# Another order of work in the lead-in of a chunked scan with a feed-forward layer, one dummy product less, and an earlier place for loads and state copies

## The chip, the cores and the metric

The kernel runs on one core of a Trainium2 chip. A core has five engines that run their own instruction lists in order and wait for each other through semaphores: TensorE (PE, matrix products; PEld is its weight load), VectorE (DVE), ScalarE (ACT), GpSimd (POOL) and SyncE (SP), which here only issues DMA transfers. The metric is the time of one execution in microseconds of the device; the median of several runs is compared.

## The reference

Per batch (4) and head (8), a sequence of 768 steps is run through a decayed linear recurrence in chunks, and its output, 3072 tokens of 256 features, goes through a feed-forward layer of width 2048.

```python
for c in range(nc):
    cum = np.cumsum(la, axis=-1)                       # la = log(a) of the chunk
    L = np.exp(cum[:, :, :, None] - cum[:, :, None, :]) * causal
    M = np.einsum('bhin,bhjn->bhij', Cc, Bc) * L
    y = M @ xc + (Cc @ state) * np.exp(cum)
    state = exp(sum(la)) * state + sum_j(Bc_j x_j * exp(cum[-1] - cum_j))
h = y_all @ w_in
out = np.maximum(0.01 * h, h) @ w_out
```

## The kernel before, in words

The sequence is cut into 16 chunks of 48 steps. For a chunk c the kernel makes the exponents of the decays on TensorE (in the buffer `pd` or `sc`), takes their exponential on ScalarE into `lt` (`decay_exp`, L290 and L295), makes the scores C·B on TensorE (`scores`, L327), multiplies the two on VectorE (`weigh`, L341), lets GpSimd write the decay of the carried state beside them (`state_decay`, L312), and then forms with 64 small products both the outputs of the chunk and its next state (`chunk_products`, L357). The state leaves by a transpose on VectorE into `stage` (`turn`, L387) and eight small copies into the input `xs` of the next chunk (`hand_on`, L403). A tuple of numbers gives the engine of each of the eight: 0 is ScalarE, 1 VectorE, 2 GpSimd. So each chunk waits for the copies of the one ahead of it.

The exponents of chunks 0 to 2 are made directly from `la` (`fill_reach`, L591, on VectorE; `decay_direct`, L263). From chunk 3 on they come from one product (`decay_stack`, L271) of two stacked tables, `dl` and `dr`. Some of their rows are sums of `la`, split into three parts (`split_sums`, L223 to L228), written to DRAM (`save_sums`, L231 and L235) and read back for each chunk (`load_rows`, L244 and L247); the upper rows of `dr` are filled once (`fill_rest`, L203).

The feed-forward layer needs each output in a high and a low part (`highs` on ScalarE, `lows` on VectorE), 512 tokens at a time, and each weight block in a high part `wh` and a low part `wl`. A weight block arrives raw by DMA (`fetch_w`), and five steps make it: `mag` on ScalarE (`decode_abs`, L441), `decode_hold` and `decode_shift` on VectorE (L453, L458), `decode_sign` (L464) and `decode_low` (L473) on VectorE, then `settle`: `wh` on ScalarE (L486) and `wl` on GpSimd (L487). `ahead` runs the next block's `mag` early. The six products of a feed-forward step (`ffn_in`, L518) take the pairs in this order: `xh` with `wh`, `xl` with `wh`, `xh` with `wl`. Then ScalarE and VectorE make the activation and its low part (L525, L528, L531), and a later `ffn_out` (L542) multiplies by the second weights. Step 0 starts when chunk 2's outputs and weight block 0 are there. Steps 1 and 3 carry chunks 3 and 4; they are the ones with `s < EARLY` in the main loop that hand a state on.

The order of all work is that of the Python code: the engines take their instructions in the order in which the code issues them. `keep_warm` (L120) issues dummy products: `WARM` of them at the start and four more ahead of step 1. SP's queue holds a load back until the buffer or the transfer that it needs is free, and everything behind it waits too.

Of the kernel before, what the change touches and what calls it, by code (L numbers as in the profile page):

```python
# [10 lines left out]
F32 = mybir.dt.float32  # L11
# [21 lines left out]
WARM = 4  # L33
# [30 lines left out]
def scan_ffn(ctx: ExitStack, tc: tile.TileContext, a_l, c_l, d_l, x_l, w_l, out_l):  # L64
# [73 lines left out]
    fetch_x(2)  # L138
# [62 lines left out]
    def fill_rest():  # L201
        both = [Q, SLOTS * NM, Q]
        nc.vector.tensor_copy(  # L203
            dr[:Q].rearrange("q b m i -> q (b m) i"), later[:Q].unsqueeze(1).to_broadcast(both)
        )
# [183 lines left out]
    def hand_on(c, by):  # L389
        if c + 1 == NC:  # L390
            return
        stage = stages.pop(c)
        alloc_x(c + 1)
        pairs = [slice(0, 2), slice(2, NB)]
        for g in range(2):
            for p in range(2):
                rows = slice((2 * g + p) * D, (2 * g + p) * D + N)
                for k, bs in enumerate(pairs):
                    copy = (nc.scalar.copy, nc.vector.tensor_copy, nc.gpsimd.tensor_copy)[
                        by[4 * g + 2 * p + k]  # L400
                    ]
                    h = half(g, bs.start)
                    copy(  # L403
                        xss[c + 1][h * R:h * R + N, 2 * p:2 * p + 2, bs], stage[rows, :, bs],
                    )
# [165 lines left out]
    with tc.tile_pool(name="ps_d", bufs=2, space=PSUM, reuse_waits="tile") as ps_d:  # L571
# [26 lines left out]
        def reverse_near(space, at):  # L598
            for k in range(2):
                for g in range(2):  # L600
# [4 lines left out]
                    )  # L605
            nc.scalar.activation(
# [15 lines left out]

        fill_columns()
# [8 lines left out]
        fill_reach(2, 0)  # L632
# [3 lines left out]
        fill_reach(1, 0)  # L636
        next(splitting)
        for _ in splitting:
            pass
        fill_reach(1, 1)  # L640
        save_sums(0)
        load_rows(3)
        load_rows(4)
        fetch_c(3)
# [3 lines left out]
        reverse_near(first, 2 * Q)  # L648
        decay_direct(1, pds[1])
        state_decay(0)  # L650
        weigh(0, sc)
        spread_c(1)
# [3 lines left out]
        for top in tops:  # L656
            nc.gpsimd.memset(top.rearrange("p c h -> p (c h)").bitcast(F32), 0.0)
# [10 lines left out]
        fill_rest()  # L668
# [8 lines left out]
        fetch_w(1, nc.scalar)  # L677
        state_decay(2)
        lows(0, os)
        os = banks()  # L680
# [6 lines left out]
        fetch_x(3)  # L687
        fetch_w(2)
# [18 lines left out]
        state_decay(3)  # L707
# [3 lines left out]
        turn(2, os)  # L711
        decode_abs(2)
# [3 lines left out]
        hand_on(2, (0, 2, 0, 2, 0, 2, 0, 0))  # L716
        decode_hold(2)
        decode_shift(2)
        weigh(3, scs[3])
# [172 lines left out]
    for s in range(total):  # L892
# [29 lines left out]
        if c is not None:  # L922
            os = banks()
            chunk_products(c, os)
            if s < EARLY:
                turn(c, os)
            else:
                states(c, os)
# [11 lines left out]
        if c is not None:  # L940
            highs(c, os)
            if s < EARLY:
# [5 lines left out]
                hand_on(c, (0, 2, 0, 2, 0, 2, 0, 2))  # L948
# [33 lines left out]
        if s == 0:  # L982
            fetch_x(LEAD + 1)
# [98 lines left out]
```

## Time and profile before

| what | us |
|---|---|
| three runs | 307.56, 307.9, 370.02 |
| median | 307.9 |
| the profiled execution | 307.64 |
| its span in the trace | 305.3 |
| TensorE busy in the span | 295.8 |
| VectorE, ScalarE, GpSimd busy | 221.5, 182.4, 71.9 |

The span runs from the first to the last recorded instruction; 2.3 us of the profiled execution lie around it. Busy times are sums over the whole span, in which stages differ much: TensorE is busy without a break through most of it, and with breaks in its first 45 us. The granted clock of TensorE is given in tenths of full speed (2.4 GHz; the lower level is 1.2 GHz).

### The profile page before, as it was taken

The page shows a single profiled execution, that of the slowest core. Times are in us where ns is not written, and L with a number is a line of the kernel's source. Part 1 is how long each engine was busy: PE and PEld are TensorE (multiplying, and loading weights), DVE is VectorE, ACT ScalarE, POOL GpSimd, SP SyncE. Part 2 cuts the span into 40 slices and gives each one's busy share as a digit, 9 for nine tenths or more (in the row PEclk, how much of TensorE's full clock was granted, in tenths as well). Part 3 has the DMA queues.
Part 4 walks back from the last instruction along what each step waited for, and adds up shares of the span by engine and source line. Part 5 has one row for each costly group of instructions (what it writes and reads, how often), then busy time and mean ns, then how long its engine had stood idle before and what let it go on. Part 6 is the DMA issues. An engine that isn't in the chain of part 4 may idle for free.

```text
span 305.3 us, 6817 instructions
## 1 busy us (share of the span) xinstructions
PE 295.8 (97%) x2720; PEld 233.4 (76%) x2720; DVE 221.5 (73%) x395; ACT 182.4 (60%) x348; POOL 71.9 (24%) x149
## 2 busy tenths in 40 slices
PE   8879899999999999999999999999999999999994
PEld 4557677777777777888888888888888888888883
DVE  7898888978786679956877887677665565556552
ACT  7857886766755554845365556673665364536452
POOL 5735676857676430000000000000000000000000
PEclk9979999999999999999999999999999999999999
DMA  7696674585634001000100000000030000000003
GB/s 227 211 298 242 241 253 150 172 243 194 227 101 133 3 2 71 0 2 0 69 3 0 0 0 2 1 0 0 2 127 10 0 3 0 0 0 2 0 0 137
DMA packets 12428, 23.86 MB, mean 78 GB/s; under 512 B 4334, under 2 KB 4718, under 8 KB 12398
## 3 DMA queue, kind: packets, MB, share of 16 engines
q1 hardware_dynamic: 12254, 22.92, 22.3%
q10 hardware_dynamic: 144, 0.52, 0.5%
q8 instruction: 21, 0.34, 0.5%
q14 instruction: 9, 0.07, 0.1%
HBM read 20.00 MB, written 3.44 MB: 77 GB/s over the span
## 4 chain that ended last, share of the span: by engine, by line
PE 85%; POOL 3%; issue 3%; DVE 3%; ACT 2%; DMA 2%; SPq 1%; POOLq 0%; DVEq 0%; ACTq 0%
PE sc L786 18%; PE op L811 14%; PE sc L811 14%; PE op L542 13%; PE hp L518 12%; PE hp L786 7%; PE sc L357 3%; DMA bcn<-c_l 2%; PE sc L327 2%; POOL wl L487 2%; PE sc L271 1%; POOL xs L403 1%; DVE top L464 1%; ACT xs L403 1%; DVE w L473 1%
## 5 line engine op out<-in xcount | busy, mean ns | idle before, releaser
L403 POOL COPY xs<-stage 16x128 f32<-16x128 f32 x99 | 35.4, 357 | 24.8 <-DVE stage L387 16.4
L525 ACT ACTIVATE gh<-hp 128x512 fp32r<-128x512 f32 x32 | 19.1, 597 | 24.3 <-PE hp L518 24.1
L822 ACT ACTIVATE gh<-u 128x512 fp32r<-128x512 f32 x32 | 20.0, 626 | 17.7 <-DVE u L863 17.7
L542 PE MATMUL op<-gh,wh 128*128 128x512 f32 x64 | 27.9, 436 | 0.0
L826 DVE TENSOR_TENSOR gl<-u,gh 128x512 fp32r<-128x512 f32 x32 | 22.0, 687 | 7.9 <-ACT u L823 7.9
L862 DVE TENSOR_TENSOR u<-sc,kept 128x512 f32<-128x512 f32 x16 | 11.1, 692 | 22.2 <-PE sc L786 22.2
L822 ACT ACTIVATE gh<-kept 128x512 fp32r<-128x512 f32 x16 | 10.1, 632 | 28.1 <-DVE kept L871 28.1
L822 ACT ACTIVATE gh<-hp 128x512 fp32r<-128x512 f32 x16 | 9.6, 599 | 26.8 <-PE hp L786 26.8
L871 DVE TENSOR_TENSOR kept<-sc,kept 128x512 f32<-128x512 f32 x16 | 11.1, 692 | 19.5 <-PE sc L786 19.3
L542 PE MATMUL op<-gh,wl 128*128 128x512 f32 x64 | 25.1, 392 | 0.0
L542 PE MATMUL op<-gl,wh 128*128 128x512 f32 x64 | 25.0, 391 | 0.0
L531 DVE TENSOR_TENSOR gl<-hp,gh 128x512 fp32r<-128x512 f32 x32 | 21.7, 679 | 4.5 <-ACT hp L528 4.3
L811 PE MATMUL op<-gh,wh 128*128 128x512 f32 x64 | 24.9, 389 | 0.0
L811 PE MATMUL sc<-gh,wh 128*128 128x512 f32 x64 | 24.9, 389 | 0.0
L811 PE MATMUL sc<-gl,wh 128*128 128x512 f32 x64 | 24.9, 389 | 0.0
L811 PE MATMUL op<-gl,wh 128*128 128x512 f32 x64 | 24.9, 389 | 0.0
L811 PE MATMUL sc<-gh,wl 128*128 128x512 f32 x64 | 24.9, 389 | 0.0
L811 PE MATMUL op<-gh,wl 128*128 128x512 f32 x64 | 24.9, 389 | 0.0
L487 POOL TENSOR_TENSOR wl<-w,wh 128x512 fp32r<-128x512 f32 x16 | 21.1, 1320 | 11.7 <-ACT wh L486 11.4
L341 DVE TENSOR_TENSOR lt<-sc,lt 128x384 f32<-128x384 f32 x32 | 16.3, 551 | 8.9 <-ACT gh L525 7.8
L518 PE MATMUL hp<-xh,wh 128*128 128x512 f32 x64 | 20.8, 407 | 0.2 <-DVE stage L387 0.2
L823 ACT ACTIVATE u<-u 128x512 f32<-128x512 f32 x32 | 20.2, 633 | 1.0
(150 smaller groups left out, 741.6 us busy)
## 6 DMA issues: line engine op xcount, KB each, us to landing
raw<-w_l SPq DMA_DIRECT2D x15, 512.0 KB, 3.8
bcn<-d_l SPq DMA_DIRECT2D x13, 448.0 KB
xs<-x_l SPq DMA_DIRECT2D x16, 256.0 KB, 3.5
out_l<-ob SPq DMA_DIRECT2D x12, 256.0 KB, 2.0
bcn<-c_l SPq DMA_DIRECT2D x3, 352.0 KB
raw<-w_l ACTq DMA_DIRECT2D x1, 512.0 KB
dl<-left_d SPq DMA_DIRECT2D x13, 9.0 KB, 1.6
dr<-right_d SPq DMA_DIRECT2D x13, 9.0 KB
```

What stands on the lines that cost most here:

```text
L341: nc.vector.tensor_tensor(out=to, in0=at, in1=to, op=ALU.mult)
L403: copy(xss[c + 1][h * R:h * R + N, 2 * p:2 * p + 2, bs], stage[rows, :, bs],)
L487: nc.gpsimd.tensor_tensor(out=wl[:, f], in0=w32s[f], in1=wh[:, f], op=ALU.subtract)
L518: nc.tensor.matmul(hp, lhsT=w_half[h][:, f, k * 128:(k + 1) * 128], rhs=x[t][:, k, :], start=(n == 0), stop=(n == 5),)
L525: nc.scalar.activation(ghs[s], hp, AF.Prelu, alpha=0.01)
L531: nc.vector.tensor_tensor(out=gls[s], in0=hps.pop(s), in1=ghs[s], op=ALU.subtract)
L542: nc.tensor.matmul(op, lhsT=w_half[h][:, f, DM + m * 128:DM + (m + 1) * 128], rhs=x, start=(start and i == 0), stop=(last and i == 2),)
L786: nc.tensor.matmul(bank, lhsT=w[h], rhs=x[g], start=start and i == 0, stop=i == 2, skip_group_check=True,)
L811: nc.tensor.matmul(outs[t][m], lhsT=w_half[h][:, f, DM + m * 128:DM + (m + 1) * 128], rhs=x, start=start and i == 0, stop=last and i == 2,)
L822: nc.scalar.activation(gh, h, AF.Prelu, alpha=0.01)
L823: nc.scalar.activation(in_place, h, AF.Prelu, alpha=0.01)
L826: nc.vector.tensor_tensor(out=gl, in0=g, in1=gh, op=ALU.subtract)
```

## The change: what it does

- One dummy product less at the start (`WARM` 3 for 4).
- Up to the products of chunk 1, steps change places. The part of `reverse_near` that is on TensorE goes ahead of the scores of chunk 0, with its exponential (`reverse_near_exp`) behind chunk 0's decay. The second and third part of the split sums go behind, with the save of the sums. The clearing of the two `top` buffers on GpSimd goes ahead of and between two state decays. `fill_rest` goes from one copy on VectorE ahead of chunk 0's transpose to two half copies behind `lows(0)`, the one on VectorE, the other on GpSimd.
- Loads: x of chunk 2 goes behind the save, followed by the input of chunk 3 and weight block 1 (which ScalarE's queue issued before), and only then by the rows of chunks 3 and 4. x of chunk 4 goes ahead of weight block 2.
- State copies: `hand_on` takes a set of engines. For chunks 2, 3 and 4 GpSimd's four copies are issued right behind the transpose and ScalarE's four at the old place. Chunk 2 had five on ScalarE and three on GpSimd. `ahead()` (the `mag` of block 3) is called ahead of ScalarE's copies of chunk 2.

```diff
-WARM = 4
+WARM = 3
...
     fetch_c(2)
-    fetch_x(2)
...
-    def fill_rest():
-        both = [Q, SLOTS * NM, Q]
-        nc.vector.tensor_copy(
-            dr[:Q].rearrange("q b m i -> q (b m) i"), later[:Q].unsqueeze(1).to_broadcast(both)
-        )
+    def fill_rest(b, eng):
+        eng.tensor_copy(dr[:Q, b], later[:Q].unsqueeze(1).to_broadcast([Q, NM, Q]))
...
-    def hand_on(c, by):
+    def hand_on(c, by, engines=(0, 1, 2)):
...
+                    engine = by[4 * g + 2 * p + k]
+                    if engine not in engines:
+                        continue
...
+        def fill_top(i):
+            nc.gpsimd.memset(tops[i].rearrange("p c h -> p (c h)").bitcast(F32), 0.0)
...
-        fill_reach(2, 0)
+        fill_reach(1, 0)
         splitting = split_sums(first)
         next(splitting)
         spread_c(0)
-        fill_reach(1, 0)
-        next(splitting)
-        for _ in splitting:
-            pass
         fill_reach(1, 1)
-        save_sums(0)
-        load_rows(3)
-        load_rows(4)
-        fetch_c(3)
+        reverse_near(first, 2 * Q)
         sc = banks()
         scores(0, sc)
         decay_exp(0, pds[0])
-        reverse_near(first, 2 * Q)
+        reverse_near_exp(first, 2 * Q)
+        next(splitting)
+        fill_reach(2, 0)
         decay_direct(1, pds[1])
+        fill_top(0)
         state_decay(0)
+        fill_top(1)
         weigh(0, sc)
+        for _ in splitting:
+            pass
+        save_sums(0)
+        fetch_x(2)
+        fetch_c(3)
+        fetch_w(1)
+        load_rows(3)
+        load_rows(4)
         spread_c(1)
         decay_exp(1, pds[1])
         spread_c(2)
         state_decay(1)
-        for top in tops:
-            nc.gpsimd.memset(top.rearrange("p c h -> p (c h)").bitcast(F32), 0.0)
...
         fill_reach(2, 1)
-        fill_rest()
...
-        fetch_w(1, nc.scalar)
         state_decay(2)
         lows(0, os)
+        fill_rest(1, nc.vector)
+        fill_rest(0, nc.gpsimd)
...
         fetch_x(3)
+        fetch_x(4)
         fetch_w(2)
...
         settle()
-        state_decay(3)
         decode_hold(1)
         decode_shift(1)
         lows(2, os)
         turn(2, os)
+        hand_on(2, (0, 2) * 4, (2,))
+        state_decay(3)
         decode_abs(2)
         decode_sign(1)
         do_low(1)
         settle()
-        hand_on(2, (0, 2, 0, 2, 0, 2, 0, 0))
         decode_hold(2)
         decode_shift(2)
+        ahead()
+        hand_on(2, (0, 2) * 4, (0,))
...
             if s < EARLY:
                 turn(c, os)
+                hand_on(c, (0, 2) * 4, (2,))
...
                 ahead()
-                hand_on(c, (0, 2, 0, 2, 0, 2, 0, 2))
+                hand_on(c, (0, 2) * 4, (0,))
...
         if s == 0:
-            fetch_x(LEAD + 1)
             fetch_w(max(raws) + 1)
```

The order on VectorE from the tables of chunk 1 to the transpose of chunk 1, before (`reach_137` is chunk 1's table, `reach_138` chunk 2's; `dr<-later` is `fill_rest`):

```order
L591 TENSOR_TENSOR reach_138<-la,upto 112x384
L224 TENSOR_TENSOR rest<-sc,parts 128x192
L591 TENSOR_TENSOR reach_137<-la,upto 112x384
L228 TENSOR_TENSOR parts<-rest,parts 128x4x48
L591 TENSOR_TENSOR reach_137<-la,upto 112x384
L341 TENSOR_TENSOR lt<-sc,lt 128x8x48 x2
L591 TENSOR_TENSOR reach_138<-la,upto 112x384
L203 COPY dr<-later 48x1536
L387 STREAM_TRANSPOSE stage<-pd 128x256
```

and with the change (`reach_134` is chunk 1's table, `reach_135` chunk 2's):

```order
L588 TENSOR_TENSOR reach_134<-la,upto 112x384
L220 TENSOR_TENSOR rest<-sc,parts 128x192
L588 TENSOR_TENSOR reach_134<-la,upto 112x384
L588 TENSOR_TENSOR reach_135<-la,upto 112x384
L337 TENSOR_TENSOR lt<-sc,lt 128x8x48 x2
L224 TENSOR_TENSOR parts<-rest,parts 128x4x48
L588 TENSOR_TENSOR reach_135<-la,upto 112x384
L383 STREAM_TRANSPOSE stage<-pd 128x256
```

The copy into `dr` no longer stands ahead of chunk 0's transpose; the last part of the split sums stands behind the weighing of chunk 0 for ahead of it.

The order on GpSimd from the clearing of `top` to the work of weight blocks 0 to 2, before (the `lt` rows are state decays of chunks 0, 1, 2, 3, 4; the `xs` rows the state copies of chunks 0, 1, 2):

```order
L312 TENSOR_TENSOR lt<-bcn,erev 128x16x16 x2
L657 MEMSET top_167 128x512
L657 MEMSET top_168 128x512
L403 COPY xs<-stage 16x2x64 x4
L312 TENSOR_TENSOR lt<-bcn,erev 128x16x16
L403 COPY xs<-stage 16x2x64 x4
L487 TENSOR_TENSOR wl<-w_423,wh 128x512
L312 TENSOR_TENSOR lt<-bcn,erev 128x16x16
L487 TENSOR_TENSOR wl<-w_493,wh 128x512
L403 COPY xs<-stage 16x2x64 x3
L312 TENSOR_TENSOR lt<-bcn,erev 128x16x16
L487 TENSOR_TENSOR wl<-w_546,wh 128x512
```

and with the change:

```order
L623 MEMSET top_164 128x512
L308 TENSOR_TENSOR lt<-bcn,erev 128x16x16
L623 MEMSET top_165 128x512
L308 TENSOR_TENSOR lt<-bcn,erev 128x16x16
L400 COPY xs<-stage 16x2x64 x4
L308 TENSOR_TENSOR lt<-bcn,erev 128x16x16
L201 COPY dr<-later 48x768
L400 COPY xs<-stage 16x2x64 x4
L484 TENSOR_TENSOR wl<-w_425,wh 128x512
L400 COPY xs<-stage 16x2x64 x4
L308 TENSOR_TENSOR lt<-bcn,erev 128x16x16
L484 TENSOR_TENSOR wl<-w_499,wh 128x512
```

The four copies of chunk 2 now stand ahead of the `wl` of block 1, where three stood behind it; a half of `fill_rest` stands ahead of chunk 1's copies.

SP's queue behind the load of chunk 2's input (the third `bcn<-c_l`), before:

```order
L113 DMA xs<-x_l 128x512
L231 DMA left_d<-parts 128x2x144
L235 DMA right_d<-parts 128x288
L244 DMA dl<-left_d 48x2x48
L247 DMA dr<-right_d 6x16x48
L244 DMA dl<-left_d 48x2x48
L247 DMA dr<-right_d 6x16x48
L105 DMA bcn<-d_l 128x896
L244 DMA dl<-left_d 48x2x48
L247 DMA dr<-right_d 6x16x48
L113 DMA xs<-x_l 128x512
L96 DMA raw<-w_l 128x2048 x2
```

and with the change:

```order
L227 DMA left_d<-parts 128x2x144
L231 DMA right_d<-parts 128x288
L113 DMA xs<-x_l 128x512
L105 DMA bcn<-d_l 128x896
L96 DMA raw<-w_l 128x2048
L240 DMA dl<-left_d 48x2x48
L243 DMA dr<-right_d 6x16x48
L240 DMA dl<-left_d 48x2x48
L243 DMA dr<-right_d 6x16x48
L240 DMA dl<-left_d 48x2x48
L243 DMA dr<-right_d 6x16x48
L113 DMA xs<-x_l 128x512 x2
```

The input of chunk 3 (`bcn<-d_l`), x of chunk 2 and weight block 1 now stand ahead of the rows that are read back.

## Rows read from the trace of the kernel before

**Rows 1.** The page's first part: busy time of the engines in us, share of the span, instructions.

```profile
PE 295.8 (97%) x2720; PEld 233.4 (76%) x2720; DVE 221.5 (73%) x395; ACT 182.4 (60%) x348; POOL 71.9 (24%) x149
```

**Rows 2.** Busy time of each engine by stretch (stretch, its length, then PE, PEld, DVE, ACT, POOL busy with their counts, the granted clock, the share of the DMA engines, GB/s), late stretches.

```profile
33.15:36.00 2.85, 1.94 (x93) 1.53 (x96) 2.38 (x5) 2.83 (x7) 2.65 (x5) 1.00 0.98 361
...
42.30:45.00 2.70, 2.40 (x98) 1.86 (x98) 1.61 (x4) 2.67 (x7) 2.50 (x5) 1.00 0.96 344
45.00:130.00 85.00, 85.00 (x1236) 65.25 (x1235) 69.53 (x130) 54.25 (x108) 44.35 (x98) 1.00 0.37 120
```

**Rows 3.** The same view, the lead-in's second half up to feed-forward step 0.

```profile
10.00:12.00 2.00, 2.00 (x20) 0.94 (x16) 1.96 (x4) 1.84 (x5) 1.72 (x7) 1.00 0.16 43
...
14.00:16.00 2.00, 1.30 (x55) 0.69 (x50) 1.96 (x6) 1.81 (x5) 1.14 (x4) 1.00 1.01 388
16.00:18.00 2.00, 0.83 (x44) 0.51 (x33) 1.84 (x5) 1.22 (x3) 0.00 (x0) 1.00 0.86 272
18.00:20.00 2.00, 1.29 (x29) 1.13 (x29) 1.97 (x7) 0.62 (x1) 1.19 (x1) 0.82 0.83 208
20.00:22.00 2.00, 2.00 (x6) 1.37 (x5) 1.93 (x4) 0.97 (x2) 1.13 (x2) 0.50 1.00 345
```

**Rows 4.** Instructions in order of time (start, duration, engine, line, operation, tile, count; in brackets the idle time ahead and what ended it): TensorE, the dummies at the start and the first part of `reverse_near`.

```profile
1.05 1.89 PE L120 MATMUL sc<-idle 128*128 128x512 bf16 x4 [1.05 <-DVE idle L116]
...
6.95 0.31 PE L602 MATMUL sc<-la,after 48*64 48x24 f32 x8
```

**Rows 5.** The same view, VectorE from chunk 0's transpose to the end of weight block 0.

```profile
8.63 0.97 DVE L203 COPY dr<-later 48x1536 bf16<-48x1536 bf16 x1
...
9.53 0.43 DVE L387 STREAM_TRANSPOSE stage<-pd 128x256 f32<-128x256 f32 x1
...
12.06 0.56 DVE L422 TENSOR_TENSOR xl<-pd,xh 128x384 fp32r<-128x384 f32 x1
13.48 0.45 DVE L387 STREAM_TRANSPOSE stage<-sc 128x256 f32<-128x256 f32 x1 [0.86 <-PE sc L357]
...
17.32 0.69 DVE L473 SCALAR_TENSOR_TENSOR w<-raw,top 128x512 uint32<-128x512 uint32 x1
```

**Rows 6.** The same view, GpSimd.

```profile
5.34 0.40 POOL L194 COPY dl<-sel 6x256 bf16<-6x256 bf16 x1
...
9.13 1.40 POOL L657 MEMSET top<- 128x512 f32 x2
10.59 1.28 POOL L403 COPY xs<-stage 16x128 f32<-16x128 f32 x4
11.95 0.62 POOL L312 TENSOR_TENSOR lt<-bcn,erev 128x256 f32<-128x256 f32 x1
...
18.81 1.27 POOL L487 TENSOR_TENSOR wl<-w,wh 128x512 fp32r<-128x512 f32 x1 [3.48 <-ACT wh L486]
20.04 1.09 POOL L312 TENSOR_TENSOR lt<-bcn,erev 128x256 f32<-128x256 f32 x1
...
31.10 1.29 POOL L487 TENSOR_TENSOR wl<-w,wh 128x512 fp32r<-128x512 f32 x1 [3.00 <-ACT wh L486]
32.46 2.16 POOL L403 COPY xs<-stage 16x128 f32<-16x128 f32 x4
```

**Rows 7.** The same view, ScalarE.

```profile
10.08 0.80 ACT L306 ACTIVATE cs<-bcn,mine 128x192 f32<-128x192 f32 x2 [1.07 <-DMA bcn<-c_l]
...
18.05 0.62 ACT L486 CAST wh<-w 128x512 fp32r<-128x512 f32 x1 [0.33 <-DVE w L473]
...
21.71 0.62 ACT L486 CAST wh<-w 128x512 fp32r<-128x512 f32 x1 [0.93 <-DVE w L473]
22.24 1.57 ACT L403 COPY xs<-stage 16x128 f32<-16x128 f32 x5
...
25.06 0.66 ACT L441 ACTIVATE mag<-raw 128x512 bf16<-128x512 bf16 x1
```

**Rows 8.** The same view, TensorE: chunk 3's scores, the first pair of feed-forward step 0, the last pair of step 1, chunk 4's products.

```profile
17.14 0.38 PE L327 MATMUL sc<-bcn 32*64 32x96 f32 x4 [0.69 <-DMA bcn<-d_l]
18.52 0.88 PE L327 MATMUL sc<-bcn 32*64 32x96 f32 x28 [1.00 <-issue]
...
19.58 1.19 PE L518 MATMUL hp<-xh,wh 128*128 128x512 f32 x2 [0.18 <-DVE stage L387]
...
24.62 0.63 PE L518 MATMUL hp<-xh,wl 128*128 128x512 f32 x2
...
34.33 1.12 PE L357 MATMUL sc<-lt,xs 64*32 64x64 f32 x56 [0.86 <-POOL xs L403]
```

**Rows 9.** The same view, DMA issues (their duration is the issue's).

```profile
11.05 0.32 SPq L244 DMA_DIRECT2D dl<-left_d  x1
...
12.63 0.36 SPq L105 DMA_DIRECT2D bcn<-d_l  x1
```

**Rows 10.** The page's DMA parts: the queue that carries the engines' code (packets, MB, share of 16 engines), and the loads of the `dl` rows (count, KB each, median us from issue to landing).

```profile
q8 instruction: 21, 0.34, 0.5%
...
dl<-left_d SPq DMA_DIRECT2D x13, 9.0 KB, 1.6
```

**Rows 11.** VectorE in order of time, two `decode_sign` (L464): the first with GpSimd idle, the second beside the GpSimd row at 31.10.

```profile
28.83 0.74 DVE L464 SCALAR_TENSOR_TENSOR top<-raw,mag 128x512 uint16<-128x512 uint16 x1
...
31.75 1.25 DVE L464 SCALAR_TENSOR_TENSOR top<-raw,mag 128x512 uint16<-128x512 uint16 x1
```

More of the change, by code (lines that the diff above doesn't have):

```diff
@@ L387, in turn @@
         nc.vector.transpose(stage, by_batch(c, space)[:, :, :, :D])
-    def hand_on(c, by):
+    def hand_on(c, by, engines=(0, 1, 2)):
         if c + 1 == NC:
             return
-        stage = stages.pop(c)
+        stage = stages[c]
         alloc_x(c + 1)
@@ L398, in hand_on @@
                 for k, bs in enumerate(pairs):
-                    copy = (nc.scalar.copy, nc.vector.tensor_copy, nc.gpsimd.tensor_copy)[
-                        by[4 * g + 2 * p + k]
-                    ]
+                    engine = by[4 * g + 2 * p + k]
+                    if engine not in engines:
+                        continue
+                    copy = (nc.scalar.copy, nc.vector.tensor_copy, nc.gpsimd.tensor_copy)[engine]
                     h = half(g, bs.start)
@@ L605, in reverse_near, with reverse_near_exp @@
                     )
+        def reverse_near_exp(space, at):
             nc.scalar.activation(
```

## Prediction

> **What bounds the kernel now.** The first view is the page's busy times: TensorE works in 295.8 of 305.3 us, the others far less [rows 1]. So the question is where its 9.5 us of idle time lie. The second view, stretches, answers: from 45 us on TensorE has no break (85.00 of 85.00 us in the first 85) [rows 2]. No order of work shortens that part; the end moves by what the first 45 us give. Idle time that is left there: 0.91 us between 33.15 and 36, 0.30 between 42.3 and 45 [rows 2], and 6.00 - 1.30 - 0.83 - 1.29 = 2.58 between 14 and 20 [rows 3]. Behind that last idle stretch the granted clock falls to 0.50, the lower of its two levels, in 20 to 22, with 0.82 in the two microseconds ahead [rows 3]; that costs 2 x 0.50 + 2 x 0.18, about 1.4. These large pieces together are 5.2 us. Two per cent of the time, about what a measurement of this kernel can tell from no change, are 6.2. So even a change that won all of them would stay within 2%.
>
> The third view, instructions in order of time, tells what TensorE waits for. In the lead-in it waits for chunk 3's input (0.69) and then, inside 32 products of one kind, 1.00 us for nothing that the profile shows [rows 8]. Step 0 then begins at 19.58 [rows 8], though its `wh` is there at 18.67 [rows 7]. In chunk 4's products it waits for GpSimd's state copies (0.86) [rows 8], which stand behind the `wl` of 31.10, which waited for ScalarE [rows 6]. Behind both is one chain: VectorE makes a weight block, ScalarE its `wh`, GpSimd its `wl`.
>
> The sum is made against the profiled execution, 307.64 us, 0.26 under the median of the three runs.
>
> **The change part by part.**
>
> *One dummy less.* 1.89 / 4 = 0.47 us [rows 4]. Ahead of chunk 0's scores now stand the small `reverse_near` products, 0.31 [rows 4]. At most 0.16 us is left, and the scores wait for ScalarE besides. I take 0.
>
> *VectorE without `fill_rest` ahead of the transpose.* The copy runs from 8.63 to 9.60 and chunk 0's transpose right behind it [rows 5]. That transpose can come a few tenths earlier, but ScalarE then still waits for chunk 2's input until 10.08 [rows 7], whose transfer has the same bytes ahead of it as before, and so `xl` of chunk 0 still comes at 12.06. What can be gained shows at chunk 1's transpose: VectorE is free for it at 12.06 + 0.56 = 12.62, now does its half of the copy (0.97 / 2 = 0.49) and can transpose at 13.11, where it did at 13.48 after a wait for TensorE [rows 5]. TensorE makes chunk 1's products earlier, since GpSimd's copies of chunk 0 (10.59 to 11.87) lose the two clearings (1.40) ahead of them and can follow the transpose at once [rows 6]. Gain 0.37, and VectorE works on without much idle time to the end of weight block 0 at 18.01 [rows 5], which becomes 17.64. Bounds 0 and 0.37.
>
> *GpSimd's half of `fill_rest`.* 768 elements a lane: by the copy of 256 of the same type (0.40) 1.2 us, by the slowest operation on 256 (1.09) 3.3 [rows 6]. The state decay of chunk 2 ahead of it ends at about 11.5 (12.57 less the 1.0 by which chunk 0's copies come earlier). So it ends between 12.7 and 14.8; chunk 1's copies can begin at 13.56. Cost 0 to 1.2; I take 0, by the row of the same type.
>
> *Loads.* Rows for chunk 3 were asked for at 11.05, when the DMA engines stood at 0.16 [rows 3, 9]. Now 256 KB of x, 448 KB of chunk 3's input and 512 KB of weights are ahead in the queue: 1216 KB at the 388 GB/s of a full stretch [rows 3] are 3.1 us. If these begin at about 10.5 (the save now follows the weighing of chunk 0), they end at 13.6, and the rows land between 14.2 and 15.2 (1.6 us from issue to landing [rows 10] is the upper end). Chunk 2's products need the short product from them and began at 15.26. Cost 0 to 0.5; I take 0. In return chunk 3's input, asked for at 12.63 [rows 9], is asked for near 10: the 0.69 of waiting at 17.14 goes. That alone moves no later step, since step 0 waits for the weight block: `wh` at 18.67 - 0.37 = 18.3. What x of chunk 4 adds ahead of weight block 2 is 256 KB, 0.7 us, and the earlier transfers give that back.
>
> *State copies of chunk 2 on GpSimd, ahead of block 1's `wl`.* Block 0's `wl` ends at 20.08 - 0.37 = 19.71. Then four copies (1.28 to 2.16), a state decay (0.62 to 1.09) and `wl` (1.27) [rows 6] end between 22.9 and 24.2. Step 1's last pair needed it at 24.62 [rows 8]. Behind the waiting `wl` is nothing but the next state decay. Cost 0.
>
> *ScalarE.* From 21.71 on it works without idle time in front of these rows, and one copy of five goes: 1.57 / 5 = 0.31 [rows 7]. Block 3's `mag` (0.66) comes ahead of the other four, which then end near 23.8 as before; chunk 3's products came after step 1's last pair, so the 0.66 is covered by it, and if step 1 ended before 23.8 they would be what is late next. Gain 0.31, bounds 0 and 0.31.
>
> *State copies of chunks 3 and 4.* GpSimd stood idle for 3.00 us and then did `wl` and the copies (2.16) while TensorE waited [rows 6, 8]. Now the copies fall into that idle time. Both waits, 0.91 + 0.30 = 1.21, can go, bounds 0 and 1.21. Against it: beside GpSimd's work VectorE's `decode_sign` has taken 1.25 us for 0.74 [rows 11], and the moved copies now lie where it ran alone. I put 0.2 for that, since four copies beside VectorE were themselves the slower part (2.16 for 1.28 [rows 6]): 1.0 is left. Late next is step 5's `wl`, by the same chain.
>
> The Trainium skill, GPSIMD Engine Reference, "8. Key points", says that GpSimd shares its SBUF interfaces with VectorE and contends with instructions that read two SBUF inputs. `decode_sign` has two such inputs, and the rows at 28.83 and 31.75 agree with it [rows 11]; by the rule with its full price on both moved groups, the sum would lose another 0.8 (the third rival).
>
> **Sum.** 0.37 + 0.31 + 1.0 = 1.68: 307.64 - 1.7 = **305.9 us**. With each term between its bounds, without a new wait, 305.1 to 307.4 (1.7 + 0.8 and 0.2).
>
> **The rivals.**
>
> 1. *The wait without a name stays.* The 1.00 us at 17.5 lies between two products of one kind [rows 8]; 21 code transfers bring 0.34 MB, 16 KB each [rows 10], and such a transfer under full DMA engines (0.86 and more [rows 3]) would be such a wait. If it now falls elsewhere or lasts until 18.5 again, or grows by 0.7 because loads now fill the stretch of 10 to 12, the lead-in's 0.37 is lost and the chain behind it shifts: 0.31 + 1.0 - 0.5, **306.8**. Against it: the loads are over earlier, so later code comes sooner. The Trainium skill, Runtime: NRT & Kernel Launch, "Instruction fetch mechanics", calls the crossing of a 16 KiB block mostly hidden; by that the gap would be something else and this rival void. The row shows 1.00 us that is not hidden.
>
> 2. *Slower: the rows for chunk 3 come late.* If they land after 15.2 instead of 14.2 to 15.2, the short product holds TensorE's queue, and with it chunk 2's products, its outputs, block 1's `mag` behind them on ScalarE, and so VectorE. Landing at 16.5 (if the loads take the 272 GB/s of 16 to 18 [rows 3], 1216 KB need 4.5 us, and 1.6 comes on top: 10.5 + 4.5 + 1.6) means chunk 2's products at 17.0, 1.7 late. Of that 0.37 + 0.9 (step 0's spare time from 18.67 to 19.58) are absorbed on TensorE, but VectorE's transpose and `decode_sign` move from 19.4 to about 20.5; chunks 3 and 4 then find the chain 1.1 late and their waits stay: 307.64 + 1.1 - 0.3 = **308.4**.
>
> 3. *GpSimd and VectorE in each other's way.* Two `decode_sign` that ran alone take 0.51 longer each, 1.0 in all, and weight blocks 3 and 5 come that much later: the gain from the copies is gone, 307.64 - 0.7 = **306.9**. For it: rows 11. Against it: 1.25 beside the `wl` of 31.10 may come from that operation alone, not from copies of 16 lanes.
>
> 4. *The clock holds.* With chunk 3's input early, TensorE's idle time of 2.58 between 14 and 20 shrinks; if the clock then stays at its upper level, 1.4 more could come, and step 1 is limited only by `wl` at 22.9. Then 305.9 - 0.4 (fewer half-clock products ahead of step 1) - 1.4 = **304.1**. Against it: step 0 still waits for `wh`, and much idle time remains.
>
> **How the numbers follow.** Forecast (305.1 to 306.6) 0.44; rival 1 0.17; rival 3 0.12; rival 2 0.12; rival 4 0.12; something else 0.03. The predicted time is the forecast's, 305.9. The range from 303.9 to 307.9 takes in the forecast, its bounds and rivals 1, 3 and 4 (0.85) and leaves out rival 2 and the rest. Faster by over 2% means under 301.5, which needs more than all idle time and clock that the first 45 us hold: 0.02. Slower by over 2% is three times and more what rival 2 costs: 0.02. Within: 0.96.
>
> **What would show it.** In the changed kernel: chunk 1's transpose at about 13.1 and block 0's `w` at 17.6 (the 0.37); no wait for chunk 3's input; the product from `dl` and `dr` of chunk 3 before 15.2 (else rival 2); a gap inside a run of equal small products (rival 1); `wl` of block 1 before 24.2; TensorE without a wait for GpSimd between 33 and 45 (the 1.2) and `decode_sign` at 0.74 or 1.25 beside the moved copies (rival 3); the granted clock behind 18 us (rival 4). The prediction is wrong if TensorE waits after 45 us, or if the lead-in gains whole microseconds that VectorE's chain was said to forbid.

## The result and the profile after

The changed kernel took 311.6 us (median of 4 runs, 311.0 to 313.7) beside 308.8 for the kernel before: ratio 1.0112, 95% interval 1.0074 to 1.0149. The ratio leaves out one slow execution of the kernel before, of 370.02 us, which its median of 308.8 takes in. The change is slower by 1.1%, inside the 2% that the prediction gave 0.96 to, but outside its range of times and on the other side: the forecast was a gain of 1.7 us. The profiled executions stand 311.5 to 307.64 us, spans 309.5 to 305.3.

The page's busy times of the changed kernel, as in [rows 1]:

```profile
span 309.5 us, 6820 instructions
...
PE 295.1 (95%) x2719; PEld 231.4 (75%) x2719; DVE 220.0 (71%) x395; ACT 182.2 (59%) x347; POOL 72.8 (24%) x151
```

TensorE works 0.7 us less in a span that is 4.2 longer, so its idle time grew by 4.9. The stretches say where, as in [rows 2, 3] (stretch, length, busy time of each engine with its count, granted clock, share of the DMA engines, GB/s):

```profile
12.00:14.00 2.00, 1.07 (x59) 0.79 (x42) 1.51 (x6) 1.94 (x7) 0.88 (x3) 1.00 0.93 310
14.00:16.00 2.00, 0.00 (x0) 0.00 (x0) 1.87 (x6) 0.48 (x1) 0.66 (x3) 0.70 0.88 301
16.00:18.00 2.00, 0.16 (x1) 0.13 (x2) 1.42 (x2) 0.00 (x0) 0.00 (x0) 0.50 0.04 13
18.00:20.00 2.00, 2.00 (x74) 1.24 (x76) 0.00 (x0) 1.06 (x3) 0.00 (x0) 0.50 0.04 5
...
45.00:130.00 85.00, 84.62 (x1319) 63.94 (x1318) 68.72 (x132) 55.69 (x114) 46.78 (x100) 1.00 0.43 138
```

Between 13 and 18 us TensorE does nothing, the granted clock falls to 0.50 four microseconds earlier than before, and from 16 the DMA engines are all but idle too. From 45 us on TensorE is again close to full, with 0.38 us of idle time in these 85 us where the kernel before had none [rows 2]: nearly all of the loss lies in the lead-in. Instructions of TensorE in order of time, as in [rows 8], chunk 2's scores to step 1:

```profile
12.18 0.89 PE L323 MATMUL sc<-cs,bcn 32*64 32x96 f32 x32
17.84 0.82 PE L267 MATMUL pd<-dr,dl 102*128 102x384 bf16 x2 [4.77 <-DMA dl<-left_d]
18.59 1.19 PE L353 MATMUL pd<-lt,xs 64*32 64x64 f32 x64
19.71 1.56 PE L323 MATMUL sc<-bcn 32*64 32x96 f32 x32
22.73 0.70 PE L515 MATMUL hp<-xh,wh 128*128 128x512 f32 x2 [1.47 <-DVE stage L383]
...
26.70 0.72 PE L515 MATMUL hp<-xh,wh 128*128 128x512 f32 x2 [1.12 <-ACT wh L483]
```

The short product waits 4.77 us for the rows of chunk 3, and step 0 begins at 22.73 where it was 19.58 [rows 8]. SyncE's loads in order of time, as in [rows 9], from the save of the sums to these rows:

```profile
8.71 0.39 SPq L227 DMA_DIRECT2D left_d<-parts  x1
...
10.55 0.43 SPq L113 DMA_DIRECT2D xs<-x_l  x1
11.12 0.34 SPq L105 DMA_DIRECT2D bcn<-d_l  x1
11.51 0.43 SPq L96 DMA_DIRECT2D raw<-w_l  x1
12.03 0.38 SPq L240 DMA_DIRECT2D dl<-left_d  x1
```

The view of the tile `dl` has one such load between 9 and 18 us:

```profile
DMA to landing us min/median/max: 5.8/5.8/5.8
```

That was 1.6 us [rows 10]. ScalarE then shows what the delay does next (block 1's and block 2's `mag`, and block 1's `wh`):

```profile
20.38 0.66 ACT L438 ACTIVATE mag<-raw 128x512 bf16<-128x512 bf16 x1
20.95 0.60 ACT L483 CAST wh<-w 128x512 fp32r<-128x512 f32 x1
25.48 0.66 ACT L438 ACTIVATE mag<-raw 128x512 bf16<-128x512 bf16 x1 [3.93 <-DMA raw<-w_l]
```

Block 1's `mag` stands behind chunk 2's outputs, and block 2's waits 3.93 us for its weights, which SyncE asked for only at 20.36 (15.81 before), since the rows of chunk 5 ahead of them on its queue wait for chunk 3's short product.

### The profile page after: what moved, and what is told of

The parts are those of the page before. It is cut to its first block, busy times and chain, and to the rows that moved or that the text cites. A ratio compares the mean times of both kernels' runs of the same rounds, so it can differ in the third digit from the quotient of the medians.

```text
span 309.5 us, 6820 instructions
## 1 busy us (share of the span) xinstructions
PE 295.1 (95%) x2719; PEld 231.4 (75%) x2719; DVE 220.0 (71%) x395; ACT 182.2 (59%) x347; POOL 72.8 (24%) x151
## 4 chain that ended last, share of the span: by engine, by line
PE 86%; ACT 5%; DMA 4%; DVE 2%; issue 1%; SPq 1%; DVEq 0%; ACTq 0%
PE sc L794 18%; PE op L819 14%; PE sc L819 14%; PE op L539 13%; PE hp L515 12%; PE hp L794 7%; PE sc L353 3%; PE sc L323 2%; DMA dl<-left_d 2%; DMA raw<-w_l 2%; PE sc L267 1%; ACT xs L400 1%; ACT gh L522 1%; ACT lt L291 1%; ACT mag L438 1%
## 5 line engine op out<-in xcount | busy, mean ns | idle before, releaser
L400 POOL COPY xs<-stage 16x128 f32<-16x128 f32 x100 | 36.1, 361 | 25.2 <-DVE stage L383 18.9
```

What stands on the lines that cost most here:

```text
L400: copy(xss[c + 1][h * R:h * R + N, 2 * p:2 * p + 2, bs], stage[rows, :, bs],)
```

## The experiments

Ratios are to the kernel before on the same chip, with their 95% intervals.

**The large loads.** First the change with its loads back at their old place:

```diff
+    fetch_x(2)
...
-        fetch_x(2)
-        fetch_c(3)
-        fetch_w(1)
         load_rows(3)
         load_rows(4)
+        fetch_c(3)
...
+        fetch_w(1, nc.scalar)
```

> The change with every load at its old place (x of chunk 2 early, rows of chunks 3 and 4 right behind the save, then the input of chunk 3, weight block 1 on ScalarE's queue, x of chunk 4 after step 0). Theory Q (all of the loss is the rows of chunk 3 behind 1216 KB, and SP's queue held behind them): no wait of 4.8 us ahead of the product from dl and dr, that product before 14.5, step 0 before 19.6, time 306.8 to 307.8. Rival R (the moved engine steps and state copies cost the time): 310 or more.

Measured: 310.2 us, 1.0064 (1.0041 to 1.0088). Better than the change, but the time is rival R's (310 or more) and not theory Q's. The wait for `dl` is gone; TensorE waits 2.7 us for chunk 3's input instead, and in this profile chunk 0's scores took 1.56 us where they take 0.89 at the upper clock level. So the loads are only a part. The other way round, the kernel before with these loads alone (the diff with its signs turned, and `fetch_x(4)` beside `fetch_x(3)`):

> The kernel before with the loads alone in the change's order. Theory Q: the product from dl and dr of chunk 3 waits 3 us or more for its rows, step 0 after 21.5, time 310 to 312. Rival R: 307.5 to 308.5.

Measured: 310.8 us, 1.0092 (1.0064 to 1.0119), as theory Q has it: most of the loss, though the save is early here (6.74). Its waits of TensorE:

```profile
PE sc L356 <- issue: 2.3, 1, 2.3
...
PE pd L270 <- DMA dl<-left_d: 0.6, 1, 0.6
```

The longest is not the wait for rows. It has no releaser, and in order of time it lies inside 64 equal products of chunk 1:

```profile
11.80 1.06 PE L356 MATMUL sc<-lt,xs 64*32 64x64 f32 x41
15.12 0.42 PE L356 MATMUL sc<-lt,xs 64*32 64x64 f32 x23 [2.27 <-issue]
```

The rows are late all the same: they land 6.5 us after their issue at 10.59, so at 17.1, when the short product starts. Without the break it would have stood ready about 2.3 us earlier (an estimate from the row above) and waited for the same rows. The one wait hides most of the other.

**Rows ahead of two loads, in the change.** Chunk 2's x stays ahead of the rows, chunk 3's input and the weight block go behind them:

```diff
         fetch_x(2)
-        fetch_c(3)
-        fetch_w(1)
         load_rows(3)
         load_rows(4)
+        fetch_c(3)
+        fetch_w(1)
```

> The change with the rows of chunks 3 and 4 ahead of the input of chunk 3 and weight block 1 in SP's queue; only the 256 KB of x stay ahead of them. Theory Q: rows asked for near 11.5 land before 14.3, the wait of 4.8 us shrinks to under 0.7, chunk 3's input is late again (about 17), time 307 to 308.3. Rival R: 310 or more.

Measured: 310.4 us, 1.0064 (1.004 to 1.0087), again rival R's time. No wait for `dl`; waits of 1.8 us for VectorE's transpose and 1.0 for chunk 3's input in its place.

**The state copies alone**, in the kernel before:

```diff
-        hand_on(2, (0, 2, 0, 2, 0, 2, 0, 0))
...
+        hand_on(2, (0, 2) * 4, (2,))
...
+                hand_on(c, (0, 2) * 4, (2,))
...
-                hand_on(c, (0, 2, 0, 2, 0, 2, 0, 2))
+                hand_on(c, (0, 2) * 4, (0,))
```

> The kernel before with the state copies of chunks 2 to 4 alone in the change's order. Theory S (from 24 to 48 us a loop through ScalarE and VectorE of 8.5 us per chunk sets the pace, and TensorE's waits for GpSimd are its spare time): the waits for GpSimd's copies go, the distance from chunk 4's products to chunk 5's stays 8.4 to 8.6, time within 0.4 of before. Rival, the forecast's term: 0.8 to 1.2 us less than before.

Measured: 307.8 us, 0.9989 (0.9966 to 1.0011): nothing, or little. In the view of waits, TensorE's for `xs` are down to one:

```profile
PE sc L357 <- POOL xs L404: 0.3, 1, 0.3
```

(The one that is left is in chunk 1's products.) So the waits went, as the prediction said, and the time did not. Theory S named a sign that did not come, a distance of 8.4 to 8.6 us from chunk 4's products to chunk 5's (TensorE in order of time):

```profile
34.33 0.86 PE L357 MATMUL sc<-lt,xs 64*32 64x64 f32 x64
...
42.01 0.86 PE L357 MATMUL sc<-lt,xs 64*32 64x64 f32 x64
```

That is 7.68. In this profile TensorE had waited 3.11 us for chunk 3's input and began step 0 at 20.76, 1.18 later than in the kernel before; without waits for copies it caught up. ScalarE kept the pace of theory S, 8.51 us from one `gh` to the next but one (33.09 to 41.60).

**The dummy.** The change, then the change with the loads back, each with four dummies again, and the kernel before with three:

```diff
-WARM = 3
+WARM = 4
```

> The change with the fourth dummy product back; loads and state copies stay as changed. Theory L (the loads alone make the change slower; the dummy is worth nothing, as the forecast had it): 311.0 to 312, as the change. Theory D (with three dummies TensorE comes up to its upper level in the lead-in late in most executions, at about 13 us and not at about 5, which the median shows; with four it is early in all): 309.5 to 310.7, and the first scores at 0.89 us in the profile. Both: the wait for dl of chunk 3 stays at 3 to 5 us.

Measured: 312.1 us, 1.0124 (1.0099 to 1.015). Above both ranges, and nearer to theory L's: the fourth dummy gives the change nothing back, and the first scores took 1.55 us here. The short product waited 3.90 us.

> The change with all loads at their old place and the fourth dummy back: what is left is the lead-in's other orders and the state copies. Theory D with L: both costs gone, so 306.5 to 308.3, no wait for dl, first scores at 0.89 us. Theory L without D: as the same kernel with three dummies, 309.5 to 310.9. A third theory (the lead-in's orders themselves cost about 2 us, whatever the dummies): also 309.5 to 310.9, but with first scores at 0.89 us.

Measured: 309.1 us, 1.0021 (0.9993 to 1.005), between the theories. First scores at 0.89, but a wait that none had named. SyncE's loads in order of time:

```profile
8.48 0.39 SPq L228 DMA_DIRECT2D left_d<-parts  x1
8.91 0.47 SPq L232 DMA_DIRECT2D right_d<-parts  x1
12.38 0.32 SPq L241 DMA_DIRECT2D dl<-left_d  x1
12.81 0.32 SPq L244 DMA_DIRECT2D dr<-right_d  x1
```

ScalarE's queue in the same stretch:

```profile
12.31 0.41 ACTq L96 DMA_DIRECT2D raw<-w_l  x1
```

and TensorE:

```profile
16.51 0.80 PE L268 MATMUL pd<-dr,dl 102*128 102x384 bf16 x2 [2.77 <-DMA dr<-right_d]
```

The change also moved the last part of the sums' split behind chunk 0's weighing. The save is issued at 8.48 in place of 6.73, the rows at 12.38 in place of 11.05 [rows 9], and ScalarE asks for weight block 1 at 12.31: even with the old order of loads the rows are now asked for just behind 512 KB of another queue. They land 4.3 us after their issue, for 1.6 before [rows 10].

> The kernel before with three dummy products in place of four, nothing else changed. Forecast's term (dummy worth nothing): 308.0 to 308.9, equal to before. Theory D: 309 to 310.8, a wider spread among executions, and where the profile fell on a late one the first scores at about 1.56 us in place of 0.89 and chunk 1's products done at about 15.5 in place of 13.4 us.

Measured: 308.95 us, 1.0022 (1.0 to 1.0045), between the two ranges. The profiled execution has the first scores at 1.56.

**The held queue.** In the change the rows of chunk 5 go behind x of chunks 3 and 4 and weight block 2:

```diff
-        load_rows(5)
         fetch_x(3)
         fetch_x(4)
         fetch_w(2)
+        load_rows(5)
```

> The change with the rows of chunk 5 queued behind x of chunks 3 and 4 and weight block 2 on SP, so that these no longer stand behind the wait for the decay product. Theory Q2 (the held queue makes the second delay, the wait of 3.93 us of ScalarE's mag for weight block 2): that wait goes, weight block 2 is read by about 22 us, and the time is 310.0 to 311.0. Theory that the second wait hides behind the first and behind the recurrence of the state copies: 311.0 to 312, though the wait goes. Both: TensorE's wait for dl of chunk 3 stays at 4 to 5 us.

Measured: 310.6 us, 1.008 (1.0053 to 1.0107). The wait of 3.93 is gone, the wait for `dl` is 3.2, and the time is theory Q2's. The second hold costs up to about 1 us, though the interval overlaps the change's own.

**The late save.** First the change with split and save early, then the kernel before with both late, then the change with dummy, loads and save as before:

```diff
+        next(splitting)
+        for _ in splitting:
+            pass
         fill_reach(1, 1)
+        save_sums(0)
+        fetch_x(2)
+        fetch_c(3)
+        fetch_w(1)
+        load_rows(3)
+        load_rows(4)
...
-        next(splitting)
         fill_reach(2, 0)
...
         weigh(0, sc)
-        for _ in splitting:
-            pass
-        save_sums(0)
-        fetch_x(2)
-        fetch_c(3)
-        fetch_w(1)
-        load_rows(3)
-        load_rows(4)
```

The loads and the rows keep their order behind the save and so come earlier with it.

> The change with the split of the sums and their save where the kernel before has them, ahead of chunk 0's scores; three dummies, the loads ahead of the rows and the state copies stay as changed. Theory V (the save is late, and the rows with it; the large loads then run ahead of them): the save at about 7, the large loads over by about 14, rows of chunk 3 landed by 14 to 15.5, the wait for dl gone or under 1 us, time 308.3 to 309.8 (the dummy's 0.8 left). Theory L (large loads ahead of the rows are what makes them late, wherever the save stands): wait for dl of 2 us and more, 310.5 to 312.

Measured: 309.75 us, 1.005 (1.0028 to 1.0071), as theory V has it. No wait for `dl` although the same loads are ahead of the rows; a wait without a releaser appears in TensorE's order of time, as in the kernel with the loads alone:

```profile
13.08 0.68 PE L353 MATMUL sc<-lt,xs 64*32 64x64 f32 x42
14.94 0.42 PE L353 MATMUL sc<-lt,xs 64*32 64x64 f32 x22 [1.19 <-issue]
```

But an early save is not enough for early rows. The kernel with the loads alone has the same queue at the same times (rows asked for at 10.59, here 10.51), and its rows took 6.5 us to land where these took 4.0. What differed is a DMA engine that lagged behind the others, described with the prediction's first step below; how often one does the single profiles do not tell.

> The kernel before with the split of the sums, their save and the rows behind it where the change has them; four dummies, loads in the old order. Theory V: save at about 8.5 to 9 in place of 6.73, rows issued at about 12.3 in place of 11.05 and so behind weight block 1 on ScalarE's queue, landed at 16 to 16.7, a wait of TensorE for dl or dr of 1 to 3 us, time 308.9 to 310. Theory L: rows are small and the old order has no large load ahead of them on SP, so no wait and 307.9 to 308.6.

Measured: 309.3 us, 1.0031 (1.0006 to 1.0056), as theory V has it. In its profile, where the clock rises late, the wait for `dr` is 2.44 us, with rows issued at 13.41. The late save alone costs about 1 us (0.2 to 1.7).

> The change with dummy, loads and the place of the split and the save all as before: what is left are the lead-in's other orders (both halves of fill_rest, the clearings, the order of the reach rows and of the reverse products) and the state copies. Theory V: no wait for dl or dr, 307.2 to 308.2, no slower than before. Theory of the lead-in's other orders: they cost something themselves, 308.8 to 309.8.

Measured: 308.0 us, 0.9999 (0.9977 to 1.0022), as the theory of the late save has it: the lead-in's other orders and the state copies neither win nor lose. It ties with the kernel before; no version here beats it.

**More dummies**, six in the kernel before:

```diff
-WARM = 4
+WARM = 6
```

> The kernel before with six dummy products in place of four. Theory D as it now stands (the moment at which TensorE's upper level comes in the lead-in varies among executions, near 4 to 5 or near 13 us, and more dummies make the early one likelier): executions above 309 become rarer than the 6 of 25 of the kernel before, median 307.7 to 308.6 (two more products of 0.47 us push the sums back by up to 0.9, most of it beside VectorE's work). If dummies do not bear on it: the same share of executions above 309, or more, and 308.2 to 309.2.

Measured: 308.6 us, 1.0012 (0.9988 to 1.0037); 3 of 12 executions above 309 (5 of 32 in the kernel before), so not rarer. Inconclusive for the clock. It helps with the wait without a name. Chunk 3's scores, with six dummies:

```profile
17.45 0.34 PE L327 MATMUL sc<-bcn 32*64 32x96 f32 x2 [0.84 <-DMA bcn<-d_l]
19.12 1.55 PE L327 MATMUL sc<-bcn 32*64 32x96 f32 x30 [1.33 <-issue]
```

and with three:

```profile
17.02 0.38 PE L327 MATMUL sc<-bcn 32*64 32x96 f32 x5
18.55 0.87 PE L327 MATMUL sc<-bcn 32*64 32x96 f32 x27 [1.15 <-issue]
```

With four the break came after 4 products [rows 8]. So it moves by one product for each dummy more or less: its place is fixed in TensorE's instruction stream, not in time and not in the data. Chunk 1's break does the same, after 41 products with four dummies (in the kernel before it is there too, 0.19 us long, at 12.98) and after 42 with three.

**The order of loads and rows.** The kernel with the loads alone once more, with weight block 1 behind the rows, then with all three loads behind them (the diff is of the second, against the kernel with the loads alone):

```diff
         save_sums(0)
+        load_rows(3)
+        load_rows(4)
         fetch_x(2)
         fetch_c(3)
         fetch_w(1)
-        load_rows(3)
-        load_rows(4)
```

> The kernel before with the change's loads alone, as in the earlier run, but weight block 1 behind the rows of chunks 3 and 4: 704 KB are ahead of them in place of 1216. Theory C (small transfers that TensorE needs, its code and the rows, stand behind the large loads): 512 KB less at 388 GB/s are 1.3 us, so the wait without a name inside chunk 1's products shrinks from 2.27 to 0.5 to 1.5 us, no wait for dl, time 308.8 to 310.2. Theory N (early loads cost time in some other way, whatever the order): 310.2 to 311.5, as with all three ahead.

Measured: 309.7 us, 1.0053 (1.003 to 1.0075), as theory C has it. The break, again after 2 + 39 = 41 products, shrank from 2.27 to 1.14:

```profile
12.23 0.63 PE L356 MATMUL sc<-lt,xs 64*32 64x64 f32 x39 [0.24 <-ACT xh L413]
14.00 0.53 PE L356 MATMUL sc<-lt,xs 64*32 64x64 f32 x23 [1.14 <-issue]
```

> The same with the rows of chunks 3 and 4 ahead of all three large loads (x of chunk 2, chunk 3's input, weight block 1, in this order behind them). Theory C: the code comes at about 10.5 as in the kernel before, so the wait inside chunk 1's products is 0.3 us or less; no wait for dl; chunk 2's x lands near 13.5, which may hold VectorE's and GpSimd's state copies by up to 0.5; time 307.9 to 309.0. Theory N: 310.2 to 311.5.

Measured: 309.8 us, 1.0061 (1.0037 to 1.0086), outside both. Theory C's mechanism holds, as chunk 1's 64 products run through, in TensorE's order of time, and `dl` isn't waited for:

```profile
11.74 1.26 PE L356 MATMUL sc<-lt,xs 64*32 64x64 f32 x64
```

Its price does not: x of chunk 2 was put at up to 0.5 us, and VectorE's copies waited 1.38 for it (first row), TensorE 1.91 behind them (second, in TensorE's order of time):

```profile
14.87 0.45 DVE L402 COPY xs<-stage 16x128 f32<-16x128 f32 x2 [1.38 <-DMA xs<-x_l]
```

```profile
16.16 1.19 PE L356 MATMUL pd<-lt,xs 64*32 64x64 f32 x64 [1.91 <-ACT xh L413]
```

The parts, each alone, sum to about the whole: loads 0.92, late save 0.31, dummy 0.22, the rest -0.01, together 1.4% beside the change's 1.12 (0.74 to 1.49). Each part is known to about 0.25 only, and taken out of the change they weigh otherwise: 0.48 for the loads (1.12 less 0.64), 0.62 for the late save (1.12 less 0.50), nothing for the dummy (1.12 less 1.24). What is shown is that these three together are the loss, since the change without them ties with the kernel before, and that loads and late save act on the same rows.

## Why the prediction was wrong, by its steps

**The loads, cost 0 to 0.5, taken as 0.** This is the step that failed: the order of loads alone costs 0.92%, about 2.8 us. Rival 2 named how, rows late behind large loads. The forecast had the rows landed between 14.2 and 15.2; they landed at 17.83, and the short product started at 17.84. Three parts of that term were too small. The start: x of chunk 2 was asked for at 10.55, near the forecast's "about 10.5", but its first packet moved at 11.64. The rate: by 15.5 all but 40 of the 1216 KB were on their way, 3.9 us for the forecast's 3.1. The landing: "1.6 us from issue to landing" came from a place where nothing was ahead of a row. Here ten packets of 4 KB, all of weight block 1, began only after 15.5 and ran almost one at a time until 17.17. The DMA view of the change from 16.5 to 17 us has three of them and nothing else:

```profile
DMA packets 3, 0.01 MB, mean 25 GB/s; under 512 B 0, under 2 KB 0, under 8 KB 3
```

The trace's records of single packets add the rest: of the 384 packets of the four row loads 360 had begun by 15.82, but the last twelve only from 17.18 to 17.27, right behind the weight block's last. So a mean over 16 DMA engines does not price the landing: one engine lagged behind the others, and the rows were not there before its share of them was. In the kernel with the loads alone the last packets begin at 16.51 in the same way; with the save early none is left behind (13.84). In the first two a code transfer of 16 KB (14.42 to 15.39 and 12.63 to 13.68) lies right ahead of the lagging packets, so the engine that carried it may be the late one; the records do not name the engine, and with the save early there is such a transfer too, so this is not shown. Rival 2 forecast 16.5 and 308.4; the mechanism was right, its price 0.8 us by the forecast's sum against about 4 in the trace. The forecast gave it 0.12, because it took the full stretch's 388 GB/s and that landing time.

**The late save.** The prediction used it only for the start of the loads. Alone it costs about 1 us: in the kernel before it puts the rows right behind weight block 1 on the other queue. With the change's loads it weighs more, 0.62%, though the one profile with these loads and an early save that had its rows in time met no lagging engine, which may be luck. It was a missing term.

**What stands behind the late rows.** Rival 2 said that VectorE's chain would lose 1.1. It missed that SyncE's queue is held as well: the rows of chunk 5 wait for the short product, and weight block 2 behind them is asked for 4.5 us later than before. Putting the rows last gives back up to about 1 us, though the two intervals overlap.

**The dummy, 0.** It costs 0.22% (0 to 0.45), about 0.7 us, more than the 0.16 allowed, if it is real. TensorE begins at its lower level in every profile (a dummy takes 0.47 us) and rises between 4 and 6 us, or only near 10 or near 13 (five and three profiles). With three dummies the late rise is in five of six profiles, with four in three of nine, and not in the one with six; but these are single executions, and more dummies did not shift the times. Whether the dummy itself decides stays open. The profile of the change has the early rise, so its loss has another cause.

**State copies, 1.0.** Alone they gave 0.11%, 0.3 us; the forecast's 1.0 is the far end of the interval (0.34%). The waits of TensorE went, but from chunk 3's products (28.72 now, 25.18 before) to the end of chunk 6's scores (48.22 and 44.77) it takes 19.50 us where it took 19.59. What repeats there is a chain through ScalarE, from one `gh` of a chunk to the same one of the next chunk (ScalarE of the change, in order of time):

```profile
28.89 0.60 ACT L522 ACTIVATE gh<-hp 128x512 fp32r<-128x512 f32 x1
...
37.40 0.60 ACT L522 ACTIVATE gh<-hp 128x512 fp32r<-128x512 f32 x1
```

8.51 us apart, in the kernel before the same 8.51 (32.76 to 41.27), and 8.51 again with the copies alone. So TensorE's waits for GpSimd look like slack of that chain. This is argued from the equal periods; with the copies alone TensorE ran at 7.68 us per chunk while it caught up, and no run shortens the chain itself.

The third rival's clash did not come. GpSimd of the change has the moved copies and, 3 us later, a `wl`; VectorE has one `decode_sign` beside each (all in order of time):

```profile
32.82 2.34 POOL L400 COPY xs<-stage 16x128 f32<-16x128 f32 x4
35.81 1.29 POOL L484 TENSOR_TENSOR wl<-w,wh 128x512 fp32r<-128x512 f32 x1 [0.65 <-ACT wh L483]
```

```profile
33.48 0.73 DVE L461 SCALAR_TENSOR_TENSOR top<-raw,mag 128x512 uint16<-128x512 uint16 x1
...
36.49 1.22 DVE L461 SCALAR_TENSOR_TENSOR top<-raw,mag 128x512 uint16<-128x512 uint16 x1
```

Beside the copies it takes 0.73, as when alone (and 0.73 again beside the next group, at 41.99); the 1.22 lies beside `wl` and the state decay behind it, as the prediction's own objection had it. The 0.2 that the forecast put for it was not needed.

**VectorE without `fill_rest`, 0.37.** Right in direction and too small: chunk 1's transpose came at 12.51 (forecast 13.11, before 13.48), and block 0's `w` ended at 17.45 (forecast 17.64). Of this 0.45 came from elsewhere: ScalarE had chunk 2's input at 9.63, where the forecast took the 10.08 of the kernel before [rows 7] as unmoved. VectorE of the change, in order of time:

```profile
12.51 0.43 DVE L383 STREAM_TRANSPOSE stage<-sc 128x256 f32<-128x256 f32 x1
...
16.76 0.69 DVE L470 SCALAR_TENSOR_TENSOR w<-raw,top 128x512 uint32<-128x512 uint32 x1
21.08 0.29 DVE L450 TENSOR_SCALAR mag<-mag 128x512 bf16<-128x512 bf16 x1 [3.63 <-ACT mag L438]
```

The last row shows where it is lost: VectorE waits 3.63 us for ScalarE's `mag` of block 1, and ScalarE had waited 4.26 for the short product. GpSimd's half of `fill_rest` took 0.81, under the forecast's 1.2, and cost nothing. The ScalarE term of 0.31 cannot be seen beside waits of 4 us.

**Rival 1, the wait without a name.** In the change it did not reappear: the code transfer in question came at 9.15, ahead of the large loads, and chunk 3's scores stood behind the wait for the rows anyway. But its reading as a code transfer behind full DMA engines is borne out by four things: its place moves with the number of dummies, it grows from 0.19 to 2.27 us when 1216 KB are put ahead of it, it shrinks to 1.14 with 704 KB, and it goes when none is. The code queue's transfers move along. The DMA view of the kernel before, between 10 and 11 us (transfers, MB, share of 16 engines):

```profile
q8 instruction: 1, 0.02, 6.6%
```

and of the kernel with the loads alone, between 12.5 and 13, with none between 10 and 12.5:

```profile
q8 instruction: 1, 0.02, 13.1%
```

With 704 KB ahead it lies between 11.5 and 12. The records of these transfers tie the two closely: they end at 11.53, 13.68 and 12.59, and at 13.47 in the change with the save early, and chunk 1's products go on 1.45, 1.44, 1.41 and 1.47 us later. Chunk 3's break ends 1.34, 1.36 and 1.32 us behind the end of such a transfer with four, three and six dummies. Which engine's code a transfer carries the views do not tell; that it is TensorE's is inferred from this. The Trainium skill, Runtime: NRT & Kernel Launch, "Instruction fetch mechanics", calls the crossing of a 16 KiB block mostly hidden; the 0.19 agrees, the 2.27 and the kernel before's own 1.00 [rows 8] do not.

**Rival 4** is void: the clock fell earlier, not later.

**Two sums of the prediction.** Its bounds "305.1 to 307.4" do not follow from its terms: 0 to 0.37, 0 to 0.31 and 0 to 1.21 give a gain of 0 to 1.89, so 305.75 to 307.64 and, with its costs of up to 1.2 and 0.5, more. And its 9.5 us of idle time do not all lie in the first 45 us: 5.47 do, and 4.0 lie behind 130 us, past the stretch that it looked at. Neither caused the miss.

## What to carry to other kernels

Before moving a large load forward, list the small transfers that will stand behind it (rows that go through DRAM, code), on every queue, and price them from a place in the trace where bytes are ahead of them, not from their median and not from a mean rate: what waits for a transfer waits for its slowest engine. A store whose read-back is due soon is a step on the path: moving its producer by 2 us can push the read-back behind a load that nobody moved. And a wait of the busiest engine is a gain only if no chain through other engines repeats with the same period when the wait is gone.

## What the runs showed of the hardware

A 9 KB load behind 1216 KB landed 5.8 us after its issue in the change, 6.5 in the kernel with the loads alone and 4.0 with the save early, where it takes 1.6 with nothing ahead. In the change the DMA engines' mean share was 0.06 between 16 and 17.5 us, as of one in 16: the rest of the weight block in packets of 4 KB, until 17.17, and the load's own last packets behind it.

TensorE's break inside a run of equal products ended 1.3 to 1.5 us behind the end of a 16 KB code transfer in all of the seven cases above, and chunk 1's lasted longer the more bytes of loads were put ahead of that transfer in the kernel before (0.19 us with none, 1.14 with 704 KB, 2.27 with 1216).

The views show the granted clock as 1.00 from the start, while TensorE's durations (0.47 us for a dummy, 1.56 or 0.89 for chunk 0's scores) tell the lower level at first. The trace's clock record begins with the rise itself, at 5.63 us in the kernel before, 4.54 in the change and 12.92 with its loads back, and the durations agree with it: ahead of that they are the better witness.
